# A row copy, two stack remainders and an exponential moved behind what TensorE waits for in the second FFN1 stage

## The chip, the core and the metric

The kernel runs on one core of one Trainium2 chip. The metric is the device time of one execution in microseconds, 1107.72 as the median of three runs before the change. TensorE (PE) multiplies matrices into eight banks of PSUM, VectorE (DVE) and ScalarE (ACT) do the elementwise work, GpSimd (POOL) and SyncE (SP) here mostly issue DMAs. ACT issues some DMAs too, in its own instruction order.

## The reference

The block adds attention and a feed-forward network, both on the same normalized input. Attention has 32 heads of 18 columns; each token looks at 8 tokens, at distances 0, 2, ..., 14 behind it. S is 2048, D 576 and F 4608.

```python
xn = _layernorm(x)                                   # x: (1, 2048, 576)
q, k, v = split_heads(xn @ wqkv)                     # 32 heads of 18
idx = pos[:, None] - 2 * jnp.arange(8)[None, :]      # masked where negative
logits = jnp.einsum("bhsd,bhswd->bhsw", q, k[idx]) * 18 ** -0.5
attn = softmax(logits)
o = jnp.einsum("bhsw,bhswd->bhsd", attn, v[idx])
h = xn @ w1 + b1                                     # 576 -> 4608
ffn = (relu(h) ** 2) @ w2 + b2                       # 4608 -> 576
return x + merge_heads(o) @ wo + ffn
```

## The kernel before

**Number format and blocks.** Tokens come in four blocks of 512 (0 to 3). Every fp32 operand of TensorE is split into a float32r high part, written by ScalarE (names ending in `_hi`), and the remainder, which VectorE forms by subtracting the high part (`_lo`). A product is then the sum of three matmuls: high times high and the two cross terms. FFN1 and QKV also use a Strassen-like scheme: two token blocks and two feature tiles are combined into seven products, by the names T1, T2, T3, T4, B11, B22 and B21, and rest columns go through a `left` product. Sums of weights and of inputs for it are formed beforehand.

**Order of the program.** All engines run in an order written out by hand: an engine executes its instructions in the order in which the Python code issues them, and waits at semaphores for other engines and DMAs. The order is: QKV of blocks 0 and 1; the first FFN1 stage (`phase_a(0)`: 18 pairs of feature tiles for blocks 0 and 1, with the FFN2 products of block 0 between); `phase_b0` (FFN2 of block 1, and then QKV of blocks 2 and 3, by `quads`, in four halves of 14 steps, here named (0,0), (0,1), (1,0) and (1,1)); the second FFN1 stage (`phase_a(1)`, blocks 2 and 3, with the FFN2 products of block 2), and `phase_b1` with the FFN2 products of block 3 and the end.

**One pair, `ffn_pair(s, p, work)`.** `s` is the stage and `p` the pair. It has three banks, ba, bb and bc. TensorE computes B11 into ba, ScalarE copies it into bb (L663); T1 goes into bc; T2 is added into bb, and ScalarE copies bb into `u[:, 0]` (L691). T3 is added into the same bb, so TensorE waits there for L691. ScalarE copies bb again (L723), and VectorE adds it to bc into `r1[:, 1]` (L725). VectorE's two-operand instructions are issued by a helper, so the profile puts them all on L108; this add reads `r<-p,r` there. B22 starts bc anew, so TensorE waits there for that add. B21, with its relu, stands between. `work(0)` to `work(3)` put FFN2 products (L536) of the pair before in between. In the first pair of stage 1, `work` is the function `filler`: `work(0)` issues the last quad step but one, (7,1), `work(1)` the last, (6,1), and later calls attention's output product. `splits()` issues the `_hi` and `_lo` parts of weights that the next pair needs. In pairs p > 1 of stage 1 the rest columns of several products are stacked in one tile of 32-row groups; pair p=1 prepares these stacks with `stack_hi` and `stack_lo`.

**A quad step's row.** Steps 4 to 7 each finish a row of q, k, v. `row` (L1047) lets ScalarE copy the bank into a slot of the tile `st` (L1050), of which there are four in turn, and for half of the rows VectorE adds another bank to it. A DMA then writes the slot to DRAM (L1054, `kvq<-st`), issued by ScalarE or, for rows with an add, by SyncE. The copy of a row waits until the DMA of the row four earlier has read its slot.

**Attention.** It is a generator for each pair of a block and a group of eight heads, (b, g), 17 pieces long: four times a multiply of q and k and a reduction (L387), one with the maximum and its subtraction, one with the exponential (ScalarE, L396), the sum, the reciprocal and the division, and four times a multiply with v and three adds, the last into `q`. `side(k, exp)` (L421) issues the next `k` pieces of the queue, and with `exp=False` stops ahead of an exponential. Pairs, quad steps and FFN2 loops call it at fixed places, so a piece more in one place moves every later piece of attention forward until the queue's next fixed point. Loads of k, v and q are issued by GpSimd (`fetch`, L347, at L358 and L360) as a buffer is released. When block 1's attention is done, GpSimd also loads its output in another grouping (`regroup`, L845).

Of the kernel before, what the change touches and what calls it, by code (L numbers as in the profile page):

```python
# [39 lines left out]
T1, T3, B11, T2, B22, B21, LEFT, T4 = range(8)  # L40
# [5 lines left out]
def block_kernel(ctx: ExitStack, tc: tile.TileContext, x, xt, wqkv, wo, w1, b1, w2, b2, w1l, out):  # L46
# [28 lines left out]
    half = const.tile([P, 1], F32, name="half")  # L75
# [31 lines left out]
    def tt(out, a, b, op):  # L107
        return nc.vector.tensor_tensor(out=out, in0=a, in1=b, op=op)  # L108
# [18 lines left out]
    def four(dt=F32):  # L127
        return sb.tile([P, 2, TB], dt, name="r4", bufs=4)
# [292 lines left out]
    def side(k, exp=True):  # L421

        while k > 0:
            if current[0] is None:
                if not queue or queue[0][0] not in landed:
                    return k
                name, make = queue.pop(0)
                current[:] = [make(), None, name]
            if current[1] == "exp" and not exp:
                return k  # L430
            try:
                current[1] = next(current[0])
                k -= 1
            except StopIteration:
                current[0] = None
        return 0
# [38 lines left out]
    def w1_hi(n, k):  # L475
        w1s[n, k] = mt.tile([P, 2, 4, 2 * P], F32R, name="w1s", bufs=3)
        nc.scalar.activation(w1s[n, k][:, 0], raw1[n][:, 4 * k:4 * k + 4], AF.Copy)  # L477
# [66 lines left out]
    ST, LW, LR = {}, {}, {}  # L544
# [16 lines left out]
    def stack_hi(to, v):  # L561
        nc.scalar.activation(to, v, AF.Copy)

    def stack_lo(to, v):
        rows = slice(L, 2 * L)
        tt(to[rows], v[rows], to[rows].bitcast(F32), ALU.subtract)
# [27 lines left out]
    def left_weight_hi(p):  # L594
        nc.scalar.activation(LW[p % 2], LR["w"], AF.Copy)

    def left_weight_lo(p):
        rows = slice(2 * L, P)
        tt(LW[p % 2][rows], LR["w"][rows], LW[p % 2][rows].bitcast(F32), ALU.subtract)
        load_left_weights(p + 1)  # L600
# [4 lines left out]
    def ffn_pair(s, p, work, first=False):  # L605
        b0, b1 = 2 * s, 2 * s + 1
        n = s * NP + p
# [23 lines left out]
        def left(to, f, v):  # L631
            if stacked:
                return
            for k in range(2):
                nc.tensor.matmul(to, weight(LEFT, k, f), v, start=False, stop=k == 1, skip_group_check=True)  # L635
# [45 lines left out]
            stack_hi(LR["st"][:, 0:2], LR["a"][:, 0:2])  # L681
            stack_hi(ST[T4], LR["a"][:, 3])
        if not first:
            side(1 if p == 1 else 3 if s else 2 + p % 2, s == 1)
        work(0)
        product(bb, T2, ss(2))
        own_w2 = first and s == 1
# [1 line left out]
            w2_hi()  # L689
        u = four()  # L690
        nc.scalar.activation(u[:, 0], bb, AF.Copy)  # L691
        if not first:
            left(bc, 1, x4[b1])
        work(1)
# [3 lines left out]
        def splits():  # L698
            if not own_w2:
                w2_lo()  # L700
            if not last and not s:
                w1_hi(n + 1, 0)
            if ready:
                left_weight_hi(p + 1)
            if s and p == 1:
                stack_lo(LR["st"][:, 0:2], LR["a"][:, 0:2])
                stack_lo(ST[T4], LR["a"][:, 3])
                stack_hi(ST[T1], LR["s"][:, 0])
            if not own_w2:
                w2_hi()  # L710
            if not last and not s:
                w1_lo(n + 1, 0)
            if ready:
                left_weight_lo(p + 1)
            if not own_w2:
                w2_lo()
# [6 lines left out]
        nc.scalar.activation(u[:, 1], bb, AF.Copy)  # L723
        r0, r1 = four(), four()
        tt(r1[:, 1], bc, u[:, 1], ALU.add)  # L725
        if first:
            splits()
        if not last and s:
# [297 lines left out]
    QKV_BANKS = [(2, 3, 4), (5, 6, 7)]  # L1026
    rows_out = [0]

    def quad_step(k, s, j, i):
        b0, b1, gs = 2, 3, (2 * k, 2 * k + 1)  # L1030
        a, b, c, u = [bank(n)[:, :QW] if opened is None else opened for n, opened in
                      zip((*QKV_BANKS[i], i), quad_banks[i])]
        quad_banks[i] = [a, b, c, u]
        js = slice(j * P, (j + 1) * P)

        def product(to, name, v, start=False):
            mm = [(v(0, n), ws[name][0][:, n]) for n in range(2)]
            for n in range(2):
                mm += [(v(0, n), ws[name][1][:, n]), (v(1, n), ws[name][0][:, n])]
            for n, (l, r) in enumerate(mm):  # L1040
                nc.tensor.matmul(to, l[:, js], r, start=start and n == 0, stop=n == len(mm) - 1, skip_group_check=True)  # L1041

        def left(to, f, v):
            for n in range(2):
                nc.tensor.matmul(to, v[:, js], ws[LEFT, f][:, n], start=False, stop=n == 1, skip_group_check=True)  # L1045

        def row(n, f, x, y=None):  # L1047
            st = stage[0][:, rows_out[0] % NJ]
            rows_out[0] += 1
            nc.scalar.activation(st, x, AF.Copy)  # L1050
            if y is not None:
                tt(st, y, st, ALU.add)
            to = kvq[gs[f]][:, PAD + n * TB:PAD + (n + 1) * TB].rearrange("i (p j) c -> p j i c", j=NJ)[:, j]
            (nc.sync if y is not None else nc.scalar).dma_start(to, st.rearrange("p (i c) -> p i c", c=CG))  # L1054

        ss = lambda n: lambda h, q: SS[n][:, h, q]
        if s == 1:
            product(a, B11, lambda h, q: X[b0][:, h, q], start=True)
            nc.scalar.activation(b, a, AF.Copy)
        if s == 2:  # L1060
            product(c, T1, ss(1), start=True)
        if s == 3:
            product(b, T2, ss(2))
            nc.scalar.activation(u, b, AF.Copy)
        if s == 4:
            left(c, 1, x4[b1])
            product(b, T3, ss(3))
            row(b1, 1, b, c)
        if s == 5:
            product(a, B21, lambda h, q: X[b0][:, h, 2 + q])  # L1070
            left(a, 0, x4[b0])
            row(b0, 0, a)
        if s == 6:
            product(c, B22, lambda h, q: X[b1][:, h, q])
            left(c, 1, x4["d"])
            row(b0, 1, c, u)
        if s == 7:
            product(b, T4, lambda h, q: X[b1][:, h, 2 + q])
            left(b, 0, x4[b1])
            row(b1, 0, b)  # L1080
# [3 lines left out]
    def phase_b0():  # L1084
# [99 lines left out]
                fetch()  # L1184

        steps = [(1, 0), (1, 1), (2, 0), (2, 1), (3, 0), (3, 1), (5, 0), (4, 0), (5, 1), (4, 1), (7, 0), (6, 0), (7, 1), (6, 1)]
        def quads(k, half, some):
            for n in some:
                s, i = steps[n]
                quad_step(k, s, 2 * half + i, i)  # L1190
                if n in ((2, 3, 4, 8, 10, 12), (3, 6, 10, 12), range(1, 13), (3, 6, 8, 10))[2 * k + half]:
                    side(1)
                hook(k, half, s, i)
# [5 lines left out]
        def chunks(*cs):  # L1199
            for c in cs:  # L1200
                w2_hi()
                add(b, o_ops(b, c))
                w2_lo()

        def filler(i):
            if i < 2:
                quads(1, 1, [len(steps) - 2 + i])
            if i == 1:
                load_left_rows()
                LR["w"] = sb.tile([P, 7, P], F32, name="mb")  # L1210
                load_left_weights(2)
                for g in (2, 3):
                    offer(2, g)
                for g in range(G):
                    offer(3, g)
            if i == 2:
                xr[b] = [mt.tile([P, NC - 1, TB], F32, name="h", bufs=3)]
                nc.sync.dma_start(xr[b][0], yscr)
                open_y(b)
                o_hi(b, 0), o_hi(b, 1)  # L1220
                o_lo(b, 0), o_lo(b, 1)
            if i == 2.5:
                o_hi(b, 2), o_hi(b, 3)
                chunks(0)
                o_lo(b, 2), o_lo(b, 3)
                chunks(1)
            if i == 3:
                open_left(b)
                nc.sync.dma_start(kept(b, NC - 1), yleft)
# [391 lines left out]
```

## Time and profile before

| what | value |
|---|---|
| median of three runs | 1107.72 us (1107.59 to 1108.0) |
| the profiled execution's own time | 1107.93 us |
| its span | 1106.2 us |
| granted TensorE clock in it | 1.00 |
| TensorE busy | 1096.8 us, 99% |
| VectorE busy | 912.0 us, 82% |
| ScalarE busy | 575.0 us, 52% |
| GpSimd busy | 115.4 us, 10% |
| DMA | 287.83 MB, 259 GB/s over the span |

A row of the timeline has the start in us from the beginning of the span, the length, the engine with its line (ACTq, SPq and POOLq are DMAs that this engine issues), the operation with output and input tiles, and how many instructions of one kind are put together. Brackets show how long the engine stood idle ahead of it and what released it. Lengths of matmuls overlap, so the time between two starts is what counts. In the trace, stage 0's second pair lies at about 111 to 129, the fourth half of the quads ends at 621.76, the first pair of the second stage begins there, its second pair has its add at 665.27, and the third its T3 at 680.16.

### The profile page before, as it was taken

The page shows a single profiled execution, that of the slowest core. Times are in us where ns is not written, and L with a number is a line of the kernel's source. Part 1 is how long each engine was busy: PE and PEld are TensorE (multiplying, and loading weights), DVE is VectorE, ACT ScalarE, POOL GpSimd, SP SyncE. Part 2 cuts the span into 40 slices and gives each one's busy share as a digit, 9 for nine tenths or more (in the row PEclk, how much of TensorE's full clock was granted, in tenths as well). Part 3 has the DMA queues.
Part 4 walks back from the last instruction along what each step waited for, and adds up shares of the span by engine and source line. Part 5 has one row for each costly group of instructions (what it writes and reads, how often), then busy time and mean ns, then how long its engine had stood idle before and what let it go on. Part 6 is the DMA issues. An engine that isn't in the chain of part 4 may idle for free.

```text
span 1106.2 us, 13892 instructions
## 1 busy us (share of the span) xinstructions
PE 1096.8 (99%) x4950; PEld 925.2 (84%) x4950; DVE 912.0 (82%) x1223; ACT 575.0 (52%) x809; POOL 115.4 (10%) x219
## 2 busy tenths in 40 slices
PE   9999999999999999999999999999999999999998
PEld 7998888888888888888899887888888888888887
DVE  7696979897996979999979488978988789899654
ACT  5435666556566654455344355555555555533342
POOL 4000101020020100100010200202102021000100
PEclk9999999999999999999999999999999999999999
DMA  8956987889699686866755887768686785866752
GB/s 297 329 177 234 333 309 255 296 214 372 229 244 392 220 357 214 311 247 226 259 164 169 309 263 300 259 260 308 238 315 240 267 314 205 316 208 205 280 193 81
DMA packets 100279, 287.83 MB, mean 260 GB/s; under 512 B 13288, under 2 KB 41712, under 8 KB 85488
## 3 DMA queue, kind: packets, MB, share of 16 engines
q1 hardware_dynamic: 65280, 188.15, 49.1%
q0 software_dynamic: 10544, 52.14, 12.9%
q10 hardware_dynamic: 24384, 46.64, 12.6%
q8 instruction: 39, 0.64, 0.2%
q14 instruction: 32, 0.26, 0.1%
HBM read 205.14 MB, written 81.74 MB: 259 GB/s over the span
## 4 chain that ended last, share of the span: by engine, by line
PE 89%; DVE 5%; DMA 3%; ACT 1%; issue 1%; ACTq 0%; POOL 0%; DVEq 0%; POOLq 0%; SPq 0%
PE p L536 46%; PE p L629 31%; PE p L1041 5%; PE p L635 3%; DMA kvq<-st 2%; PE p L338 1%; PE p L1401 1%; PE p L1045 1%; DVE pr L108 1%; DMA kv<-kvq 1%; DVE lg L387 1%; DVE w1r L108 1%; DVE r L108 0%; PE p L1318 0%; DVE h L108 0%
## 5 line engine op out<-in xcount | busy, mean ns | idle before, releaser
L536 PE MATMUL p<-h,w2s 128*128 128x512 f32 x2066 | 491.4, 389 | 0.1
L536 PEld LDWEIGHTS p<-h,w2s 128*128 128x128 f32 x2066 | 387.5, 188 | 81.5 <-ACT h L642 0.6
L629 PE MATMUL p<-X,w1s 128*128 128x512 f32 x864 | 219.7, 389 | 1.2 <-DVE r L108 0.9
L629 PEld LDWEIGHTS p<-X,w1s 128*128 128x128 f32 x864 | 162.0, 188 | 35.6 <-DVE r L108 1.3
L509 ACT ACTIVATE w2s<-w2r 128x640 fp32r<-128x640 f32 x164 | 120.2, 735 | 116.1 <-PE p L536 87.6
L629 PE MATMUL p<-S,w1s 128*128 128x512 f32 x648 | 164.8, 390 | 1.5 <-ACT r L691 1.5
L108 DVE TENSOR_TENSOR w2s<-w2r,w2s 128x576 fp32r<-128x576 f32 x164 | 123.4, 753 | 40.6 <-ACT w2s L509 39.8
L629 PEld LDWEIGHTS p<-S,w1s 128*128 128x128 f32 x648 | 121.4, 188 | 27.4 <-ACT r L691 2.3
L415 POOL DMA_DIRECT2D o<-q x128 | 69.2, 605 | 584.8 <-DVE q L108 582.8
L638 ACT ACTIVATE r<-r,b1t 128x512 f32<-128x512 f32 x72 | 52.0, 723 | 126.9 <-DVE r L108 125.2
L387 DVE TENSOR_REDUCE lg<-pr 128x64 f32<-128x1152 f32 x64 | 86.5, 1352 | 1.5
L108 DVE TENSOR_TENSOR pr<-lg,kv 128x1152 f32<-128x1152 f32 x64 | 86.7, 1354 | 1.3
L108 DVE TENSOR_TENSOR pr<-q,kv 128x1152 f32<-128x1152 f32 x64 | 86.6, 1353 | 0.8
L108 DVE TENSOR_TENSOR pr<-pr 128x576 f32<-128x576 f32 (+1 forms) x128 | 77.5, 605 | 3.2
L646 ACT ACTIVATE r<-r 128x1024 f32<-128x1024 f32 x72 | 76.1, 1057 | 1.2
L108 DVE TENSOR_TENSOR h<-r,h 128x1024 fp32r<-128x1024 f32 (+3 forms) x46 | 51.8, 1136 | 27.0 <-ACT r L646 18.8
L108 DVE TENSOR_TENSOR r<-p,r 128x512 f32<-128x512 f32 (+1 forms) x77 | 52.9, 688 | 20.3 <-PE p L629 9.8
L108 DVE TENSOR_TENSOR w1s<-w1r,w1s 128x1024 fp32r<-128x1024 f32 (+1 forms) x42 | 50.3, 1198 | 16.5 <-ACT w1s L477 16.4
L691 ACT ACTIVATE r<-p 128x512 f32<-128x512 f32 x36 | 21.5, 597 | 70.9 <-PE p L629 70.5
L638 ACT ACTIVATE r<-p,b1t 128x512 f32<-128x512 f32 x72 | 48.3, 672 | 0.0
L108 DVE TENSOR_TENSOR h<-h 128x1024 fp32r<-128x1024 f32 x36 | 43.9, 1220 | 4.8 <-ACT h L938 4.6
L536 PE MATMUL p<-w1s,w2s 128*128 128x512 f32 x195 | 44.7, 389 | 0.0
(193 smaller groups left out, 1174.2 us busy)
## 6 DMA issues: line engine op xcount, KB each, us to landing
w2r<-in_w SPq DMA_DIRECT2D x144, 320.0 KB, 3.4
kv<-kvq POOLq DMA_DIRECT2D x29, 1296.0 KB, 9.4
w<-w1s SPq DMA_DIRECT2D x36, 1024.0 KB, 8.4
w1s<-w ACTq DMA_DIRECT2D x34, 1024.0 KB, 7.3
h<-r SPq DMA_DIRECT2D x36, 512.0 KB, 6.3
h<-h SPq DMA_DIRECT2D x36, 512.0 KB, 4.2
w1r<-in_w SPq DMA_DIRECT2D x18, 640.0 KB, 7.7
kvq<-st ACTq DMA_DIRECT2D x48, 216.0 KB, 3.2
```

What stands on the lines that cost most here:

```text
L108: return nc.vector.tensor_tensor(out=out, in0=a, in1=b, op=op)
L338: nc.tensor.matmul(p[:, :QW], l, r, start=k == 0, stop=k == len(mm) - 1)
L387: nc.vector.tensor_reduce(out=lg[:, j * HG:(j + 1) * HG].rearrange("p a w -> p w a"), in_=pr.rearrange("p w (a d) -> p w a d", d=DH), axis ...
L415: nc.gpsimd.dma_start(rows[:, i], q[i * L:(i + 1) * L, :, a:z])
L509: nc.scalar.activation(w2s[stream[i]][:, :DE], raw2[i], AF.Copy)
L536: nc.tensor.matmul(yp[b][c], v, a, start=c not in yb[b], stop=c in last and c not in [o[0] for o in ops[i + 1:]], skip_group_check=True)
L629: nc.tensor.matmul(to, l, r, start=start and i == 0, stop=i == len(mm) - 1, skip_group_check=True)
L635: nc.tensor.matmul(to, weight(LEFT, k, f), v, start=False, stop=k == 1, skip_group_check=True)
L638: nc.scalar.activation(to, a, AF.Relu, bias=b1t[:, f:f + 1])
L646: nc.scalar.activation(r, r, AF.Square)
L691: nc.scalar.activation(u[:, 0], bb, AF.Copy)
L1041: nc.tensor.matmul(to, l[:, js], r, start=start and n == 0, stop=n == len(mm) - 1, skip_group_check=True)
```

## The change

There are three edits and one consequence of how the first is written.

1. The call of `side` ahead of T2. In stage 1, pair p=2 now gets one piece, without an exponential; it had three, with one allowed. The expression for "one piece" was `p == 1` in both stages, and is now `s and p in (1, 2)`. In stage 0, pair p=1 therefore falls to `2 + p % 2`, three pieces where it had one.
2. The row of quad step (7,1), which `filler` runs inside stage 1's first pair, is held back: its matmuls stay in place, but its copy and its DMA are issued by a new call `work(0.5)`, behind L691.
3. In stage 1's pair p=1 the two `stack_lo` calls (three VectorE instructions on 32 rows, of 1024 and 512 columns, beside others) move out of `splits()` to behind the add of `r1[:, 1]`.

```diff
         if not first:
-            side(1 if p == 1 else 3 if s else 2 + p % 2, s == 1)
+            side(1 if s and p in (1, 2) else 3 if s else 2 + p % 2, s == 1 and p != 2)
         work(0)
         product(bb, T2, ss(2))
...
         u = four()
         nc.scalar.activation(u[:, 0], bb, AF.Copy)
+        if s and first:
+            work(0.5)
...
             if s and p == 1:
-                stack_lo(LR["st"][:, 0:2], LR["a"][:, 0:2])
-                stack_lo(ST[T4], LR["a"][:, 3])
                 stack_hi(ST[T1], LR["s"][:, 0])
...
         tt(r1[:, 1], bc, u[:, 1], ALU.add)
+        if s and p == 1:
+            stack_lo(LR["st"][:, 0:2], LR["a"][:, 0:2])
+            stack_lo(ST[T4], LR["a"][:, 3])
...
         def row(n, f, x, y=None):
+            put = lambda: row_out(n, f, x, y)
+            held.append(put) if held is not None else put()
+
+        def row_out(n, f, x, y):
             st = stage[0][:, rows_out[0] % NJ]
...
         def filler(i):
-            if i < 2:
-                quads(1, 1, [len(steps) - 2 + i])
+            if i in (0, 1):
+                quads(1, 1, [len(steps) - 2 + i], None if i else held)
+            if i == 0.5:
+                held.pop()()
```

TensorE's and GpSimd's instructions keep their order. Three places show how the others move.

VectorE in stage 0's second pair, before: the end of an attention piece (`pr`, `q`), then remainders of weights, then the add into `r` that frees bc (`p` is a bank).

```order
L108 TENSOR_TENSOR pr<-pr 128x576
L108 TENSOR_TENSOR pr<-pr 128x288
L108 TENSOR_TENSOR q<-pr 128x144
L108 TENSOR_TENSOR w2s<-w2r,w2s 128x576
L108 TENSOR_TENSOR w1s<-w1r,w1s 128x1024
L108 TENSOR_TENSOR w2s<-w2r,w2s 128x576
L108 TENSOR_TENSOR r_1274<-p_1193,r_1242 128x512
```

The same place on VectorE in the changed kernel:

```order
L108 TENSOR_TENSOR pr<-pr 128x576
L108 TENSOR_TENSOR pr<-pr 128x288
L108 TENSOR_TENSOR q<-pr 128x144
L108 TENSOR_TENSOR pr<-q,kv 128x1152
L387 TENSOR_REDUCE lg<-pr 128x8x8
L108 TENSOR_TENSOR w2s<-w2r,w2s 128x576
L108 TENSOR_TENSOR w1s<-w1r,w1s 128x1024
L108 TENSOR_TENSOR w2s<-w2r,w2s 128x576
L108 TENSOR_TENSOR r_1280<-p_1193,r_1248 128x512
```

A multiply and a reduction of the next attention group now stand ahead of the weights' remainders and of the add.

ScalarE in stage 1's first pair, before (`p_4700` is the bank of step (7,1), `p_5310` is bb; the row of `w_113` is a DMA of weights):

```order
L663 ACTIVATE p_5310<-p_5309 128x512
L487 DMA w1s<-w_113 128x2048
L1050 ACTIVATE st<-p_4700 128x432
L1054 DMA kvq_98<-st 128x3x144
L691 ACTIVATE r_5344<-p_5310 128x512
L1050 ACTIVATE st<-p_4701 128x432
L723 ACTIVATE r_5344<-p_5310 128x512
```

The same place on ScalarE in the changed kernel, whose line numbers are a little higher behind the added lines:

```order
L663 ACTIVATE p_5325<-p_5324 128x512
L487 DMA w1s<-w_113 128x2048
L691 ACTIVATE r_5357<-p_5325 128x512
L1057 ACTIVATE st<-p_4728 128x432
L1061 DMA kvq_98<-st 128x3x144
L1057 ACTIVATE st<-p_4729 128x432
L723 ACTIVATE r_5357<-p_5325 128x512
```

The copy and the DMA of the held row have changed places with L691.

VectorE around the end of block 1's attention, before, in the fourth half of the quads: each quad half has four `st` adds, of its steps (4,0), (4,1), (6,0) and (6,1). The first two rows of this piece are the third half's last `st` add and the last multiply with v; the rows behind `q` belong to the fourth half and to attention (2,0).

```order
L108 TENSOR_TENSOR st<-p_4702,st 128x432
L108 TENSOR_TENSOR pr<-lg,kv 128x1152
L108 TENSOR_TENSOR pr<-pr 128x576
L108 TENSOR_TENSOR pr<-pr 128x288
L108 TENSOR_TENSOR q<-pr 128x144
L108 TENSOR_TENSOR st<-p_4690,st 128x432
L108 TENSOR_TENSOR pr<-q,kv 128x1152
L108 TENSOR_TENSOR st<-p_4701,st 128x432
L387 TENSOR_REDUCE lg<-pr 128x8x8
```

The end of block 1's attention on VectorE in the changed kernel; p_4718 takes the place of p_4690, and the first `st` add here is that of the third half's step (4,0):

```order
L108 TENSOR_TENSOR pr<-lg,kv 128x1152
L108 TENSOR_TENSOR st<-p_4718,st 128x432
L108 TENSOR_TENSOR pr<-pr 128x576
L108 TENSOR_TENSOR pr<-pr 128x288
L108 TENSOR_TENSOR q<-pr 128x144
L108 TENSOR_TENSOR pr<-q,kv 128x1152
L108 TENSOR_TENSOR st<-p_4729,st 128x432
```

And the last logit multiply of (2,0) there, between the third half's last `st` add and the fourth half's first:

```order
L108 TENSOR_TENSOR st<-p_4730,st 128x432
L387 TENSOR_REDUCE lg<-pr 128x8x8
L108 TENSOR_TENSOR pr<-q,kv 128x1152
L108 TENSOR_TENSOR st<-p_4718,st 128x432
L387 TENSOR_REDUCE lg<-pr 128x8x8
```

Block 1's last `q` add has moved ahead by three `st` adds, and the logits of (2,0), of which the first multiply stood in the fourth half, are done ahead of that half's end.

More of the change, by code (lines that the diff above doesn't have):

```diff
@@ L1027, in block_kernel, with quad_step @@
     rows_out = [0]
-    def quad_step(k, s, j, i):
+    def quad_step(k, s, j, i, held=None):
         b0, b1, gs = 2, 3, (2 * k, 2 * k + 1)
@@ L1186, in phase_b0, with quads @@
         steps = [(1, 0), (1, 1), (2, 0), (2, 1), (3, 0), (3, 1), (5, 0), (4, 0), (5, 1), (4, 1), (7, 0), (6, 0), (7, 1), (6, 1)]
-        def quads(k, half, some):
+        def quads(k, half, some, held=None):
             for n in some:
                 s, i = steps[n]
-                quad_step(k, s, 2 * half + i, i)
+                quad_step(k, s, 2 * half + i, i, held)
                 if n in ((2, 3, 4, 8, 10, 12), (3, 6, 10, 12), range(1, 13), (3, 6, 8, 10))[2 * k + half]:
@@ L1203, in chunks @@
                 w2_lo()
+        held = []
         def filler(i):
-            if i < 2:
-                quads(1, 1, [len(steps) - 2 + i])
+            if i in (0, 1):
+                quads(1, 1, [len(steps) - 2 + i], None if i else held)
+            if i == 0.5:
+                held.pop()()
             if i == 1:
```

## The prediction

> **What bounds the kernel now.** I began with the page's busy times and then asked for the waits of TensorE, since an engine that is busy 99% of the span can gain only where it stands still.
>
> ```profile
> PE 1096.8 (99%) x4950; PEld 925.2 (84%) x4950; DVE 912.0 (82%) x1223; ACT 575.0 (52%) x809; POOL 115.4 (10%) x219
> ```
>
> Of the four rows in the list of what TensorE waited for, these two are the change's stake (us in total, times, longest): two waits for L691, the copy of bb, which T3 then overwrites, and one for the add into `r`, which frees bc for B22.
>
> ```profile
> PE p L629 <- ACT r L691: 1.5, 2, 0.8
> PE p L629 <- DVE r L108: 0.9, 1, 0.9
> ```
>
> The timeline of TensorE shows where they lie (start, length, line, count, idle before), behind a piece of stage 0 that has no wait:
>
> ```profile
> 121.38 1.75 PE L536 MATMUL p<-h,w2s 128*128 128x512 f32 x7
> 122.96 1.52 PE L629 MATMUL p<-X,w1s 128*128 128x512 f32 x6
> 124.32 0.61 PE L635 MATMUL p<-x4d,w1s 128*128 128x512 f32 x2
> ...
> 628.82 0.55 PE L1045 MATMUL p<-r,x4d 128*128 128x432 f32 x2
> 630.21 1.65 PE L629 MATMUL p<-S,w1s 128*128 128x512 f32 x6 [0.85 <-ACT r L691]
> 631.70 0.70 PE L635 MATMUL p<-x,w1s 128*128 128x512 f32 x2
> ...
> 663.34 1.75 PE L536 MATMUL p<-h,w2s 128*128 128x512 f32 x7
> 666.02 1.65 PE L629 MATMUL p<-X,w1s 128*128 128x512 f32 x6 [0.93 <-DVE r L108]
> 667.51 0.62 PE L635 MATMUL p<-x4d,w1s 128*128 128x512 f32 x2
> ...
> 677.71 1.75 PE L536 MATMUL p<-h,w2s 128*128 128x512 f32 x7
> 680.16 1.66 PE L629 MATMUL p<-S,w1s 128*128 128x512 f32 x6 [0.70 <-ACT r L691]
> ```
>
> The lengths overlap, so I go by starts. Without a wait, seven matmuls of L536 take 1.58 (121.38 to 122.96) and six of L629 take 1.36 (122.96 to 124.32). The two of L1045, of 432 columns in place of 512, I put at 0.39. After a wait the six take 1.49 (630.21 to 631.70, 666.02 to 667.51), so a restart costs another 0.13.
>
> **The three gains.** First wait: T3 was due at 628.82 + 0.39 = 629.21 and came at 630.21, so 1.00, with the restart 1.13. Second: B22 was due at 663.34 + 1.58 = 664.92 and came at 666.02, so 1.10, with the restart 1.23. Third: due at 677.71 + 1.58 = 679.29, came at 680.16, so 0.87, with the restart 1.00. Sum: **3.36 us**.
>
> Does each go whole? ScalarE ahead of the two copies, from its timeline:
>
> ```profile
> 617.82 0.37 ACTq L1054 DMA_DIRECT2D kvq<-st  x1
> ...
> 628.59 0.53 ACT L1050 ACTIVATE st<-p 128x432 f32<-128x432 f32 x1 [4.46 <-DMA kvq<-st]
> ...
> 629.56 0.60 ACT L691 ACTIVATE r<-p 128x512 f32<-128x512 f32 x1 [0.44 <-PE p L1045]
> ...
> 678.58 0.42 ACT L396 ACTIVATE lg<-lg 128x256 f32<-128x256 f32 x1 [1.74 <-DVE lg L108]
> ...
> 679.53 0.58 ACT L691 ACTIVATE r<-p 128x512 f32<-128x512 f32 x1
> ```
>
> The row copy at 628.59 waited 4.46 us for its slot of `st`, whose DMA went out at 617.82, and L691 stood behind it. Put ahead of it, L691 runs as soon as T2 is done. Between T2 and T3 stand the eight matmuls of step (6,1), about 1.6 us, so T2 ends near 627.6 and L691 near 628.3, 0.9 us ahead of 629.21. The held copy then delays only its own bank, whose next use is an FFN2 product some microseconds on: cost 0, or at most its own 0.5 if that cover were gone.
>
> In the third wait the exponential at 678.58 waited 1.74 us for VectorE ahead of L691. With one piece and no exponential in p=2, L691 follows T2's last matmul, just ahead of the L536 group at 677.71, and ends near 678.3, 0.9 us ahead of its due time. Later exponentials fall in other pairs, since attention is some pieces ahead. In the list of waits, L691 appears twice, and only this once behind an exponential, so I price the others at nothing and bound each at this one's 1.0 us.
>
> VectorE before the second wait:
>
> ```profile
> 660.59 1.35 DVE L387 TENSOR_REDUCE lg<-pr 128x64 f32<-128x1152 f32 x1
> ...
> 662.64 1.82 DVE L108 TENSOR_TENSOR w1r<-w1r 32x1024 fp32r<-32x1024 f32 x2
> ...
> 665.27 0.69 DVE L108 TENSOR_TENSOR r<-p,r 128x512 f32<-128x512 f32 x1
> ```
>
> The two stack remainders are the 1.82. With these behind the add, it runs from 663.45 to 664.14, and B22 is due at 664.92: 0.8 of slack. The stacks are first multiplied in p=2, some ten microseconds on, which hides the remainders' own delay. The piece ahead of them becomes a multiply in place of L387, 1.35 like it (122.49 below).
>
> **The loss in stage 0.** The new condition asks for s=1, so stage 0's second pair falls through to three pieces where it had one. The two pieces, a multiply and a reduction, come ahead of four VectorE instructions, the last of which is the add that B22 needs:
>
> ```profile
> 115.27 1.60 DVE L108 TENSOR_TENSOR w1r<-w1r 128x512 f32<-128x512 f32 x3
> ...
> 120.76 0.68 DVE L108 TENSOR_TENSOR r<-p,r 128x512 f32<-128x512 f32 x1
> ...
> 122.49 1.35 DVE L108 TENSOR_TENSOR pr<-q,kv 128x1152 f32<-128x1152 f32 x1
> 123.88 1.35 DVE L387 TENSOR_REDUCE lg<-pr 128x64 f32<-128x1152 f32 x1
> 125.15 0.68 DVE L108 TENSOR_TENSOR r<-p,r 128x512 f32<-128x512 f32 x1
> ```
>
> VectorE is packed from 115.27 to 125, so they add 1.39 + 1.27 = 2.66 (122.49 to 125.15). The add then ends at 120.76 + 0.68 + 2.66 = 124.10. B22 started at 122.96 and now starts at 124.16 (at 666.02 it followed the add's end, 665.96, by 0.06): 1.20, with the restart **1.33 us**. The bounds are 0 and, if the add r0 behind is late as well, 2.66; I take the row's own sum.
>
> **What being ahead does to the DMAs.** By the order rows, block 1's last `q` add moves from the fourth QKV half to behind the p_4718 `st` add of the third. That row, the old place, and POOL's requests that follow:
>
> ```profile
> 598.80 0.60 DVE L108 TENSOR_TENSOR st<-p,st 128x432 f32<-128x432 f32 x1
> ...
> 612.21 0.31 DVE L108 TENSOR_TENSOR q<-pr 128x144 f32<-128x144 f32 x1
> ```
> ```profile
> 616.93 0.77 POOL L360 DMA_DIRECT2D kv<-kvq  x1
> ...
> 620.14 0.54 POOL L358 DMA_DIRECT2D q<-kvq  x1
> ...
> 672.26 0.53 POOL L360 DMA_DIRECT2D kv<-kvq  x1 [51.57 <-DVE pr L108]
> ```
>
> My estimate puts that add at 601.7 (598.80, and a multiply's lag and two adds), 10.5 sooner, so the burst of requests that began at 616.93 (v, the regrouping, q) begins at about 606.4. The load at 672.26 waited for the last logit multiply of (2,0), which the order puts ahead of the fourth half's first `st` add; it follows at about 613. What a burst does to a row's DMA, by issues (KB, us to landing: the rows issued at 616.89 and 617.82, POOL's q of 620.14, and a load of k at 583.04):
>
> ```profile
> kvq<-st SPq DMA_DIRECT2D x1, 216.0 KB, 2.4
> ...
> kvq<-st ACTq DMA_DIRECT2D x1, 216.0 KB, 10.7
> ...
> q<-kvq POOLq DMA_DIRECT2D x1, 288.0 KB, 8.6
> ...
> kv<-kvq POOLq DMA_DIRECT2D x1, 1296.0 KB, 8.0
> ```
>
> The row of 617.82 landed at 628.5, the burst's last request at 628.7: I take it that a row issued inside a burst lands when the burst ends. The burst lasted 11.8 (616.93 to 628.7) and would end at 618.2. The added load, requested at 613, would land at 621.0 by the 8.0 of its like, and at 626.2 if it only began at 618.2. Requests overlapped before, so I take a point a third of the way up, 622.6.
>
> Two row copies of the fourth half need slots whose DMAs go out at 614.69 and 616.89, inside that. The T1 product overwrites the bank of the second:
>
> ```profile
> 623.35 1.52 PE L629 MATMUL p<-S,w1s 128*128 128x512 f32 x6
> ```
>
> From 622.6 the two copies (0.53 each) end near 623.7, so T1 is 0.4 late, with the restart **0.5 us**. Bounds: 0 (landing before 622.2), and 5.0 by the 10.7 of the row above (the slower rival).
>
> The Trainium skill's page "DMA: Bandwidth & Descriptors", section "Queues, rings and completion order", says that each DMA engine takes turns between its queue rows, packet by packet. By that rule alone a small row would be served beside the burst and land well before its end; this term would be 0 and the time 1105.7. The trace speaks against an equal turn here: 10.7 us inside the burst against 2.4 at its start.
>
> **Sum.** -3.36 + 1.33 + 0.5 = -1.53. The profiled execution took 1107.93 (span 1106.2) and becomes 1106.4. The median of the runs, 1107.72, is 0.21 lower, so I predict 1106.2. A measurement of this kernel can tell about 0.2%, or 2.2 us, from no change; -1.53 lies within.
>
> **The rivals.**
>
> *The stage-0 pieces are hidden.* For it: stage 0's sixth pair has three pieces at this place and no wait:
>
> ```profile
> 183.22 1.60 DVE L108 TENSOR_TENSOR w1r<-w1r 128x512 f32<-128x512 f32 x3
> ```
> ```profile
> 193.68 1.52 PE L629 MATMUL p<-X,w1s 128*128 128x512 f32 x6
> ```
>
> Against it: there VectorE began the pair's w1r sums 10.5 us ahead of B22, here 7.7 (115.27 to 122.96), so it is 2.8 behind already, about the two pieces. Without the loss: -3.36 + 0.5 = -2.86, 1104.9. Chance 0.12.
>
> *Weights take the first wait's place.* The L635 behind T3 needs the weights that SP requested at 620.49:
>
> ```profile
> w1s<-w SPq DMA_DIRECT2D x1, 1024.0 KB, 11.1
> ```
>
> They landed at 631.6, 0.1 ahead of L635 at 631.70. If they come no sooner, L635 gains 0.1 and not 1.1: 1.0 is lost, 1107.2. The same price stands for a second exponential ahead of an L691. Against it: POOL's burst should by then be over, six us sooner than before. Chance 0.20.
>
> *The slower side: row copies hold T1.* Both copies also stand ahead of L663 and L691 in ScalarE's queue. If rows issued at 614.69 and 616.89 take the 10.7, the second lands at 627.6, its copy ends at 628.2, and T1 is 4.9 late, with the restart 5.0: -3.36 + 1.33 + 5.0 = +3.0, 1110.7. The change turns slower once the second row takes over about 7.2 us (624.1, T1 1.9 late). For it: the added load goes out just ahead of these rows. Against it: most of the burst is ten us older. Chance 0.16.
>
> That the change doesn't do what it says can't be: the order rows show L691 ahead of the copy.
>
> **How the numbers follow.** The forecast has 0.52, the rivals 0.12, 0.20 and 0.16. Faster by over 0.2%: the first rival's 0.12, and 0.15 of the forecast's, where rows land in time (-2.03) and another term is a little better: 0.27. Slower by over 0.2%: the last rival's 0.16. Within: 0.57. The range runs from 1104.7, just below the first rival, to 1108.6, the forecast with T1 2.4 us later, and leaves out most of the last rival.
>
> **What would show it.** In the profile after, TensorE's waits should hold no L691 and no `r` in stage 1, but one for `r` of some 1.2 near 123, and a short one for a row copy near 623 to 625. No wait near 123 makes the stage-0 term wrong. A wait for a weight DMA behind T3, or for L691 behind an exponential, is the second rival; one of 4 us or more ahead of T1 is the third. What would make all of it wrong is an attention schedule that, some pieces ahead, collides in a place that I haven't priced.

## The result, and the profile after

The changed kernel takes 1109.51 us (median of 18 runs, 1108.22 to 1113.55) against 1107.59 for the kernel before in the same rounds (18 runs, 1106.72 to 1108.55). The ratio is 1.0021, 95% interval 1.0014 to 1.0028: **slower by 1.5 to 3.1 us**, just at the bound of 0.2%. The prediction was 1106.2 with a range up to 1108.6, so the time lies above it, and the kernel became slower where a gain of 1.5 was forecast. The profiled execution took 1110.06, its span is 1108.4.

TensorE's waits in the changed kernel:

```profile
PE p L1329 <- DVE lg L1322: 2.1, 1, 2.1
PE p L629 <- DMA w1s<-w: 1.2, 1, 1.2
PE p L536 <- DVE w2s L108: 1.2, 1, 1.2
PE p L629 <- DVE r L108: 1.2, 1, 1.2
PE p L629 <- ACT st L1057: 0.6, 1, 0.6
PE p L662 <- ACT st L1057: 0.2, 1, 0.2
PE p L536 <- ACT h L941: 0.2, 1, 0.2
```

All three waits that the change aimed at are gone: no L691 is left, and the one `r` is another one. In their place stand six new ones (the first row is the opening's, and the kernel before has it too). The timeline of TensorE shows where, and also the three places that gained:

```profile
120.33 1.75 PE L536 MATMUL p<-h,w2s 128*128 128x512 f32 x7
123.23 1.66 PE L629 MATMUL p<-X,w1s 128*128 128x512 f32 x6 [1.16 <-DVE r L108]
...
477.33 23.04 PE L536 MATMUL p<-h,w2s 128*128 128x512 f32 x99 [0.17 <-ACT h L941]
...
546.90 2.56 PE L536 MATMUL p<-h,w2s 128*128 128x512 f32 x10 [1.22 <-DVE w2s L108]
...
625.90 1.66 PE L629 MATMUL p<-X,w1s 128*128 128x512 f32 x6 [1.24 <-DMA w1s<-w]
627.81 0.49 PE L662 MATMUL p<-X,w1s 128*128 128x512 f32 x1 [0.25 <-ACT st L1057]
628.86 1.65 PE L629 MATMUL p<-S,w1s 128*128 128x512 f32 x6 [0.56 <-ACT st L1057]
...
634.46 0.55 PE L1048 MATMUL p<-r,x4d 128*128 128x432 f32 x2
634.84 1.52 PE L629 MATMUL p<-S,w1s 128*128 128x512 f32 x6
...
667.71 1.75 PE L536 MATMUL p<-h,w2s 128*128 128x512 f32 x7
669.30 1.52 PE L629 MATMUL p<-X,w1s 128*128 128x512 f32 x6
...
680.86 1.75 PE L536 MATMUL p<-h,w2s 128*128 128x512 f32 x7
682.44 1.52 PE L629 MATMUL p<-S,w1s 128*128 128x512 f32 x6
```

T3 now follows L1048 by 0.38, and the L536 groups are followed after 1.59 and 1.58: no wait. The places where time was lost are stage 0's second pair (123), block 1's FFN2 loop (477 and 547), and the start of the second stage (624 to 629).

To add them up I compare the start of the same matmul in both traces. The table compares one execution of each kernel. Their openings differ (the first L1401 matmul at 7.66 before, its twin at 7.04 after), and just ahead of the first place the changed kernel is 1.04 ahead, so only changes of the difference count:

| place | before | after | difference | lost (+) or gained |
|---|---|---|---|---|
| B22, then x4d, stage 0 pair 1 | 122.96, 124.32 | 123.23, 124.73 | -1.04 ahead of it, +0.41 behind | +1.45 |
| first QKV step of blocks 2 and 3 | 546.56 | 549.30 | +2.74 (from +0.24 at 417.59) | +2.50 |
| first product of stage 1 | 621.76 | 625.90 | +4.14 | +1.40 |
| the step behind T1 | 624.71 | 630.35 | +5.64 | +1.50 |
| L635 behind T3 | 631.70 | 636.20 | +4.50 | -1.14 |
| x4d, stage 1 pair 1 | 667.51 | 670.66 | +3.15 | -1.35 |
| stack product behind T3, pair 2 | 681.66 | 683.80 | +2.14 | -1.01 |

Losses 6.85, gains 3.50; with the opening's -1.04 and a drift of -0.17 ahead of 417.59, the difference ends at +2.14, and the span grew by 2.2.

The sources lie in the other engines' timelines. In the FFN2 loop it is a load and the weights beside it: `w2r` is loaded, ScalarE forms its high part, and VectorE the remainder in `w2s`. Here are GpSimd's load, the high part, its remainder, and the last remainder of the loop, in the changed kernel and then in the kernel before:

```profile
458.44 0.54 POOL L360 DMA_DIRECT2D kv<-kvq  x1 [42.65 <-DVE w2s L108]
466.29 0.74 ACT L509 ACTIVATE w2s<-w2r 128x640 fp32r<-128x640 f32 x1 [6.45 <-DMA w2r<-in_w]
467.06 0.76 DVE L108 TENSOR_TENSOR w2s<-w2r,w2s 128x576 fp32r<-128x576 f32 x1 [3.73 <-ACT w2s L509]
546.10 1.42 DVE L108 TENSOR_TENSOR w2s<-w2r,w2s 128x576 fp32r<-128x576 f32 x2
```
```profile
534.65 0.54 POOL L360 DMA_DIRECT2D kv<-kvq  x1 [66.45 <-DVE pr L108]
463.78 0.74 ACT L509 ACTIVATE w2s<-w2r 128x640 fp32r<-128x640 f32 x1 [4.18 <-DMA w2r<-in_w]
464.55 0.76 DVE L108 TENSOR_TENSOR w2s<-w2r,w2s 128x576 fp32r<-128x576 f32 x1 [0.75 <-ACT w2s L509]
542.97 1.42 DVE L108 TENSOR_TENSOR w2s<-w2r,w2s 128x576 fp32r<-128x576 f32 x2
```

With attention ahead, a load of 1.3 MB that stood at 534.65 goes out at 458.44, while a w2r is under way. That w2r, requested at 455.17, took 11.0 us; its counterpart, requested at 454.93, took 8.7. From there on VectorE's remainders are 2.3 to 2.5 late, and in the loop's last rounds, where adds and multiplies of attention stand in place of the maximum, the exponential and the sum, the lag grows to 3.1 (546.10 against 542.97). TensorE stands until 546.90.

For the start of stage 1, here are GpSimd's requests, ScalarE, and the landings of the weights requested at 612.98, of the row issued at 617.43 and of the load of 615.38, all after:

```profile
608.60 0.76 POOL L360 DMA_DIRECT2D kv<-kvq  x1
...
613.63 0.54 POOL L358 DMA_DIRECT2D q<-kvq  x1
615.38 0.54 POOL L360 DMA_DIRECT2D kv<-kvq  x1 [1.20 <-DVE pr L108]
```
```profile
627.22 0.53 ACT L1057 ACTIVATE st<-p 128x432 f32<-128x432 f32 x1 [5.12 <-DMA kvq<-st]
627.78 0.37 ACTq L1061 DMA_DIRECT2D kvq<-st  x1
628.27 0.53 ACT L1057 ACTIVATE st<-p 128x432 f32<-128x432 f32 x1 [0.52 <-ACT st L1057]
```
```profile
w1s<-w SPq DMA_DIRECT2D x1, 1024.0 KB, 12.9
...
kvq<-st ACTq DMA_DIRECT2D x1, 216.0 KB, 9.7
...
kv<-kvq POOLq DMA_DIRECT2D x1, 1296.0 KB, 10.9
```

The weights landed at 612.98 + 12.9 = 625.9, where the first product starts. The row issued at 617.43 landed at 627.1, 0.9 behind the load that landed at 626.3, and the next one, issued at 619.64, at 627.4. The two copies at 627.22 and 628.27 let L662 and then T1 go, with a DMA that ScalarE issues between them. The copies don't wait for the weights, and the second ends at 628.80, so T1 would have come at 628.86 with weights in time too: the table's 1.40 and 1.50 are one loss of 2.9, and the rows set it.

### The profile page after: what moved, and what is told of

Same layout as the page of the kernel before. It is cut to its first block, busy times and chain, and to the rows that moved or that the text cites. A ratio compares the mean times of both kernels' runs of the same rounds, so it can differ in the third digit from the quotient of the medians.

```text
span 1108.4 us, 13891 instructions
## 1 busy us (share of the span) xinstructions
PE 1097.2 (99%) x4950; PEld 924.7 (83%) x4950; DVE 912.6 (82%) x1223; ACT 575.2 (52%) x809; POOL 115.9 (10%) x219
## 4 chain that ended last, share of the span: by engine, by line
PE 91%; DVE 4%; DMA 3%; issue 1%; ACT 1%; ACTq 0%; POOL 0%; DVEq 0%; POOLq 0%
PE p L536 42%; PE p L629 32%; PE p L338 7%; PE p L1044 5%; PE p L635 3%; DMA w2r<-in_w 1%; PE p L1048 1%; DVE w2s L108 1%; DMA kvq<-st 1%; PE p L1412 1%; DMA h<-r 0%; DVE pr L108 0%; DVE h L108 0%; DVE w1s L108 0%; DVE r L108 0%
## 5 line engine op out<-in xcount | busy, mean ns | idle before, releaser
L536 PE MATMUL p<-h,w2s 128*128 128x512 f32 x2066 | 492.3, 389 | 1.5 <-DVE w2s L108 1.2
L536 PEld LDWEIGHTS p<-h,w2s 128*128 128x128 f32 x2066 | 387.2, 188 | 84.1 <-DVE w2s L108 2.0
L629 PE MATMUL p<-X,w1s 128*128 128x512 f32 x864 | 219.5, 389 | 2.4 <-DMA w1s<-w 1.2
L629 PEld LDWEIGHTS p<-X,w1s 128*128 128x128 f32 x864 | 162.0, 188 | 36.7 <-DMA w1s<-w 1.6
L629 PE MATMUL p<-S,w1s 128*128 128x512 f32 x648 | 164.6, 389 | 0.6 <-ACT st L1057 0.6
L629 PEld LDWEIGHTS p<-S,w1s 128*128 128x128 f32 x648 | 121.5, 188 | 25.9 <-ACT st L1057 0.9
L691 ACT ACTIVATE r<-p 128x512 f32<-128x512 f32 x36 | 21.5, 598 | 73.1 <-PE p L629 73.1
L536 PE MATMUL p<-w1s,w2s 128*128 128x512 f32 x195 | 44.7, 389 | 0.0
```

Of the source, the lines that this page charges most:

```text
L536: nc.tensor.matmul(yp[b][c], v, a, start=c not in yb[b], stop=c in last and c not in [o[0] for o in ops[i + 1:]], skip_group_check=True)
L629: nc.tensor.matmul(to, l, r, start=start and i == 0, stop=i == len(mm) - 1, skip_group_check=True)
```

## The experiments

My theory after this result: the three edits do what they were meant to, and all that is lost comes from stage 0's second pair having three pieces instead of one, a little directly and most through attention being ahead. The rivals, for the experiments as a whole, were that one of the edits loses something itself, and that the pieces only cost where they stand. Each kernel was run against the kernel before in the same rounds; ratios with 95% intervals.

**e1_one_piece**, the changed kernel with stage 0 as it was:

```diff
-            side(1 if s and p in (1, 2) else 3 if s else 2 + p % 2, s == 1 and p != 2)
+            side(1 if p == 1 or s and p == 2 else 3 if s else 2 + p % 2, s == 1 and p != 2)
```

> The changed kernel with one piece of attention again in stage 0's second pair, all three edits kept. Theory (the two extra pieces cause every loss: directly at 123, by a DVE lag near 547, and by GpSimd's earlier loads near 626): the list of TensorE's waits holds none of the six new ones, and only the gains stay, about 3.4 us under the kernel before, 1104.2, ratio 0.997. Rival (the weights that SP requests at 620.49 take the first wait's place): a DMA wait of some 1 us behind T3, 1105.2. Rival (one of the three edits itself loses): above 1107.

Measured: 1105.46 against 1107.9, ratio 0.9977 (0.9968 to 0.9986). Behind the opening's wait, and beside one of 0.2 for `h` near 112, its list holds:

```profile
PE p L635 <- DMA w1s<-w: 0.9, 1, 0.9
```

None of the six is left, so the one expression makes the difference between +0.21% and -0.23%. But the first rival of its expectation holds too: the wait for the weights behind T3 takes the first wait's place. They were requested at 619.68 and took 11.1 us, as in the kernel before.

**e3_given_back** and **e4_ahead_in_pair2** part the direct loss from being ahead:

```diff
 e3
+            side(1 if s and p in (1, 2) else 3 if s else 0 if p == 2 else 2 + p % 2, s == 1 and p != 2)
 e4
+            side(1 if p == 1 or s and p == 2 else 3 if s else 4 if p == 2 else 2 + p % 2, s == 1 and p != 2)
```

> The changed kernel with three pieces in stage 0's second pair and none ahead of T2 in its third, so that attention is level with the kernel before from the third pair on. Theory (being ahead, not the two pieces themselves, costs most): only the wait of 1.2 near 123 is left, gains 3.4 less 1.4, about 1105.6. Rival (the lag of VectorE from the second pair goes on by itself): waits in the following pairs and near 547 stay, 1108 or more.

> The changed kernel with one piece in stage 0's second pair and four ahead of T2 in its third, so that attention is as far ahead from there on as in the changed kernel, but not by pieces at 118 to 121. Theory: no wait of 1.2 near 123 (at most 0.8 one pair later), and the losses near 477, 547 and 626 stay, about 1.4 under the changed kernel, 1108.1 to 1108.9. Rival (the pieces in the second pair cause all by themselves): 1104.2.

Measured: e3 1107.39, ratio 0.9994 (0.9986 to 1.0003); e4 1110.21, ratio 1.0018 (1.0009 to 1.0027). TensorE's timeline in e3, the rows with a wait at the two places, and e4's waits:

```profile
124.34 0.97 PE L629 MATMUL p<-X,w1s 128*128 128x512 f32 x3 [1.13 <-DVE r L108]
...
633.53 0.74 PE L635 MATMUL p<-x,w1s 128*128 128x512 f32 x2 [1.06 <-DMA w1s<-w]
```
```profile
PE p L629 <- DMA w1s<-w: 1.4, 1, 1.4
PE p L536 <- DVE w2s L108: 1.2, 1, 1.2
PE p L629 <- ACT st L1057: 0.6, 1, 0.6
PE p L536 <- ACT h L941: 0.4, 1, 0.4
```

With attention level again, only the direct wait is left, and e1's wait for weights, which explains most of what e3 lies above the expected time. With attention ahead by the same two pieces, but put into the next pair, the direct wait is gone and the others are there but for the short one of L662. So being ahead makes these waits, and by the table it is the larger part: 5.4 of 6.85. The time of e4 was not as expected: it should have been some 1.4 under the changed kernel, and by its ratio it can't be told from it. Its runs spread from 1108.25 to 1111.93, and the profiled one, 1108.98, is among the shorter ones.

**e2_three_only**, the kernel before with the three pieces alone:

```diff
-            side(1 if p == 1 else 3 if s else 2 + p % 2, s == 1)
+            side(1 if s and p == 1 else 3 if s else 2 + p % 2, s == 1)
```

> The kernel before with three pieces in stage 0's second pair and none of the three edits. Theory (the pieces alone cost all): waits of 1.2 near 123, about 0.2 and 1.2 near 477 and 547, and 2 near 626 for weights and row copies, as in the changed kernel; the waits for r and for L691 behind the exponential stay in stage 1, perhaps moved, and the one for L691 near 630 goes, since T1 comes late. 4 to 6 above the kernel before, 1111.8 to 1114. Rival (part of the loss comes from the edits): 1109.5 or less.

Measured: 1112.75, ratio 1.0048 (1.0036 to 1.006), 4.0 to 6.6 slower. Its waits of the same kinds:

```profile
PE p L629 <- DVE r L108: 2.4, 2, 1.3
...
PE p L536 <- DVE w2s L108: 1.2, 1, 1.2
PE p L629 <- DMA w1s<-w: 1.0, 1, 1.0
```

With two more for the row copies, of 0.5 and 0.4, the pieces alone make every loss. One of the two waits for `r` is the new one near 123; the other stands one pair later than before, at 689. The waits for L691 are gone as well, though no edit is in. For the one behind the exponential this was not expected: with attention ahead the exponential runs at 652.89, long before the third pair's L691 at 681.52. In the changed kernel it runs at 652.86, so there, too, being ahead would have removed that wait; whether the third edit does more there, at 689, was not tested.

**e7_held_only, e8_stack_only, e9_exp_only**, each of the three edits alone on the kernel before (e9's line is e1's):

```diff
 e7
+        if s and first:
+            work(0.5)
 e8
+        if s and p == 1:
+            stack_lo(LR["st"][:, 0:2], LR["a"][:, 0:2])
+            stack_lo(ST[T4], LR["a"][:, 3])
 e9
+            side(1 if p == 1 or s and p == 2 else 3 if s else 2 + p % 2, s == 1 and p != 2)
```

> The kernel before with the held row copy alone. Theory: the wait for L691 near 630 goes, and a wait of about 0.9 for the weights of L635 takes its place, so 0.1 to 0.3 is gained, 1107.6. Rival (my sum): 1.1 is gained, 1106.8.

> The kernel before with the two stack remainders moved alone. Theory: the wait for r near 666 goes and nothing comes for it, 1.2 gained, 1106.7. Rival (the remainders delay what stands behind them): a new wait in that pair or the next, 1107.4 or more.

> The kernel before with one piece and no exponential in pair 2 of stage 1 alone, stage 0 as before. Theory: the wait for L691 near 680 goes and no other exponential costs, 1.0 gained, 1106.9. Rival (the exponential only costs elsewhere, in a later pair): a wait for L691 in a later pair, 1107.9.

Measured: e7 1108.06, ratio 1.0 (0.9991 to 1.0008); e8 1106.3, ratio 0.9986 (0.9977 to 0.9995); e9 1107.43, ratio 0.9995 (0.9987 to 1.0004). In e9's list of waits the L691 of 680 is gone and none is new in stage 1; in e7's the L691 of 630 is gone, and a wait of 0.8 for the weights of L635 has come. The remainders' move gives its 1.2 (measured 0.6 to 2.5). The held copy alone gives nothing that can be told. For the exponential the trace shows the wait gone, but the interval of the time includes no change.

**e10_late_k**, the changed kernel with the loads of k (1296 KB) and q (288 KB) of (2,1) issued by SyncE behind its last row, so not within the burst:

```diff
 def regroup(b, k):
-            kept_back[0] = 0
+            kept_back[0] = 1
...
-            if kept_back[0] and not due(1):
+            if kept_back[0] and not due(1) and (1, 0) not in ob:
...
             if i == 1:
+                kept_back[0], lane[0] = 0, nc.sync
+                fetch()
+                lane[0] = nc.gpsimd
```

> The changed kernel with the load of k and q of attention (2,1) issued by SyncE behind its last row, near 636, not by GpSimd near 614. Theory (this load lengthens GpSimd's burst, and with it the landing of the first weights and of the two rows): the waits at 625.9, 627.8 and 628.9 go or shrink below 0.5 us, 2.4 to 2.9 under the changed kernel, about 1106.8. Rival (the burst's older part is enough, or the weights were late by their own request): at least 1.2 of these waits stay, 1108.4 or more.

Measured: 1108.14 (1106.67 to 1109.93), ratio 1.0004 (0.9995 to 1.0013). The start of the second stage in its trace:

```profile
625.03 0.55 PE L1048 MATMUL p<-r,x4d 128*128 128x432 f32 x2
625.41 1.52 PE L629 MATMUL p<-X,w1s 128*128 128x512 f32 x6
626.77 0.39 PE L662 MATMUL p<-X,w1s 128*128 128x512 f32 x1
627.00 1.52 PE L629 MATMUL p<-S,w1s 128*128 128x512 f32 x6
```

All three waits are gone, while those of 123 and 547 stay. So the load that the change pulls from 672 to 615, with the q that goes with it, is what made the weights and the rows late; the rest of the burst alone does not. The q was in the burst before the change too, so the load is the new part, but e10 doesn't part the two. The ratio fell by 0.0017, 1.9 us, less than the 2.4 to 2.9 that were expected, but within the intervals.

**e12_less_at_end**, the changed kernel with one piece fewer in the loop's last round:

```diff
-                    run(pieces, 2 if n > 21 else 1 + n % 2)
+                    run(pieces, 1 if n == 32 else 2 if n > 21 else 1 + n % 2)
```

> The changed kernel with one piece in place of two in the last FFN2 iteration of block 1 that calls for pieces. Theory (the wait for w2s near 547 is VectorE's own load: a multiply of 1.35 stands just ahead of that remainder): the wait of 1.2 for w2s goes, the others stay, about 1.2 under the changed kernel, 1108.5. Rival (the remainder was late by a DMA of w2r, as the one near 477): the wait stays, 1109.7.

Measured: 1113.25, ratio 1.0048 (1.0036 to 1.006). The wait for w2s is gone as expected, so VectorE's work ahead of that remainder is part of it. This doesn't rule out the late w2r, since VectorE had been late since 467, and a piece less makes up for part of that lag. The time was not as expected: by the ratios some 3 longer than the changed kernel instead of 1.2 shorter. TensorE's timeline:

```profile
626.40 0.49 PE L662 MATMUL p<-X,w1s 128*128 128x512 f32 x1
629.95 2.51 PE L629 MATMUL p<-S,w1s 128*128 128x512 f32 x6 [3.05 <-ACT st L1057]
632.25 2.09 PE L1044 MATMUL p<-h,X 128*128 128x432 f32 x6
```

One piece less put v 1.9 later, at 610.45, and the load of k 5.7 later, at 621.07, and the second row, issued at 619.54, then took 9.7 us: T1 was due at 626.63 and came at 629.95, 3.3 late. With a further 1.7, which the last section explains, this is 5.0, the price of the prediction's slower rival. The row that holds T1 is the rival's, but that the number agrees is chance: the rival had T1 4.9 late and no slower clock.

**e11_late_v, e13_weights_sooner, e14_both** start from e1_one_piece and go for its wait for weights: e11 lets SyncE load v of (2,0) behind its last row, e13 requests the weights three quad steps sooner (612.83 in place of 619.68), and e14 does both.

```diff
 e11: fetch() and filler(1)
+            if (kind, b, g) == ("k", 2, 0):
+                kept_back[0] = 2
...
-            kept_back[0] = 0
...
-            if kept_back[0] and not due(1):
+            if kept_back[0] and not due(1) and (1, 0) not in ob:
...
+                kept_back[0], lane[0] = 0, nc.sync
+                fetch()
+                lane[0] = nc.gpsimd
 e13: the hook of the fourth half
+                if (s, i) == (5, 0):
+                    w1_again(NP, 1, nc.sync)
...
-                if (s, i) == (4, 1):
-                    w1_again(NP, 1, nc.sync)
```

> e1_one_piece with the load of v of (2,0), 1296 KB, issued by SyncE behind its last row near 630 in place of GpSimd near 616. Theory (GpSimd's burst makes the weights requested at 619.7 late, which cost 0.9 behind T3): the DMA wait on L635 goes, and some 0.9 to 1.0 is gained on e1_one_piece, 1104.4, about 3.4 under the kernel before. Rival (the weights are late by the row DMAs and ScalarE's own 1 MB request): the wait stays, 1105.4.

> e1_one_piece with the second weight request of the second stage issued by SyncE two steps sooner, near 613, ahead of GpSimd's burst. Theory (the request of 619.7 was late by that burst): the DMA wait of 0.9 on L635 goes, 1.0 under e1_one_piece, 1104.5, ratio to the kernel before 0.9967. Rival (the megabyte then makes the rows late, and T1 with them): a wait for row copies near 623 in its place, 1105.5 or more.

> e1_one_piece with both remedies: the load of v of (2,0) by SyncE near 630, and the second weight request near 613. Theory (the request of 619.7 inside GpSimd's burst is all that is left of the first wait): no wait in the second stage, about 0.9 under e1_one_piece, 1104.5. Rival (TensorE's waits in the QKV and FFN2 loops vary from run to run by as much): the median is not to be told from e1_one_piece's, 1105.0 to 1105.9.

Measured: e11 1105.04, ratio 0.9975 (0.9966 to 0.9984); e13 1105.83, ratio 0.9985 (0.9977 to 0.9994); e14 1104.58, ratio 0.9972 (0.9962 to 0.9983). In all three the wait for the weights is gone from the profile. But other waits stand in the profiled executions, at places that none of these edits touches: one of 0.7 for w2s near 545 in e14, and this one in stage 0 of e11 (L631 and L693 are L629 and L691 there):

```profile
331.73 1.65 PE L631 MATMUL p<-S,w1s 128*128 128x512 f32 x6 [1.69 <-ACT r L693]
```

So both remedies take the wait away, but neither can be told from e1 by its time, for the intervals overlap. Through stage 0 and the FFN2 loop e1, e11, e13 and e14 are the same program, so the wait at 331.73 comes from the execution, or from the chip it ran on, and not from an edit. The time of e13 is the one of its rival, though no wait for row copies is in its profile. e14, 0.28% under the kernel before, has the lowest ratio of all, and beats both kernels.

## Why the prediction was wrong

**The gains** were right to about a tenth: I had 1.13, 1.23 and 1.00, and the traces differ by 1.14, 1.35 and 1.01. The first came whole in the changed kernel because attention is ahead there, as the prediction's reason against its second rival had it: GpSimd's burst is over at 626.3, and the weights requested at 623.23 took 7.8 us and landed at 631.0, 5.2 ahead of the L635 at 636.20. In e10, too, where T1 isn't late, the L635 behind T3 doesn't wait. With attention level (e1, e7) the burst is at its old place, the weights take L691's place, which is the second rival, and the first edit gives close to nothing.

**The loss in stage 0** was right: I had 1.33 near 123, and it measured 1.45, with a wait of 1.16 in the row.

**The step that failed is "What being ahead does to the DMAs"**, in two ways. First, its term was 0.5 and measured 2.9. It had the requests in the right place (my 606.4 and 613 are 608.60 and 615.38 in a trace that runs 2.5 to 2.7 later there) and the right mechanism, rows held up by the burst, but the wrong size. I put the landing a third of the way between the load alone and the load behind the whole burst, which gives that load 9.6 us. It took 10.9, and the rows landed 0.9 behind it and not with it, so they came 1.8 later than I had them (627.1 less 2.7, against 622.6). I also set the two copies behind the landing at 0.53 each and left out the DMA that ScalarE issues between them: 1.7 us in place of 1.1. So T1 came 2.8 late and not 0.4. The first product's own weights fell into the same burst and took 12.9 us where they had taken 5.0, and I had no term for them either; here their wait lies within that of the rows.

Second, the step stopped there. The same two pieces move GpSimd's load from 534.65 to 458.44, into block 1's FFN2 loop, and I had no term for that loop at all; it lost 2.5. My closing sentence had named that (a collision in a place that I hadn't priced), but neither the sum nor the chances held it. GpSimd's list of loads, followed through the whole program, could have shown it.

**The rivals.** The slower one was right in its mechanism. The second row, issued at 619.64, took 7.8 us, a little over the turning point of 7.2, but it was the first, with 9.7, and the copy and the DMA behind it that set T1. Hidden pieces in stage 0 did not occur. The rows came 0.9 behind the end of GpSimd's load, and in e10, without that load, there was no wait. The Trainium skill's rule of turns ("DMA: Bandwidth & Descriptors", "Queues, rings and completion order"), as the prediction read it, would have let the rows land well before the load's end, and they did not. That speaks against the reading more than against the rule: the trace records a row as 384 pieces of 576 bytes and the load as 128 of 10368, so equal turns need not be equal shares. No run tests that.

**What stays open.** That the load at 458.44 makes the w2r late is read from the order in time; no run moves that load alone. For it: counted from the start of the FFN2 loop (417.59 and its twins), the remainder of 464.55 comes 2.3 to 3.1 later in all five kernels with attention ahead, and in the eight others between 0.3 sooner and 0.9 later. The whole loop takes 130.9 to 132.2 us in those five kernels and 129.0 to 130.1 in the others and the kernel before. Four places make up nearly all of the 2.5: by the starts of successive matmuls, 0.227 apart without a wait, TensorE loses 0.45 near 477, 0.25 near 497, 0.17 near 542 and 1.49 near 547. A wait for `h` of 0.17 to 0.43 near 477 stands in the five kernels with attention ahead and in none of the others. The w2s waits near 545 in e11, e13 and e14 have the same form with a smaller lag: counted in the same way, their remainder of 542.97 comes 1.1 to 1.5 later than before, where it is 0.7 at most in the level kernels without this wait. What makes VectorE late in these three I don't know; e1 is the same program there and has no such wait.

## What to carry to other kernels

Where side work is dealt out in pieces, one piece more in one place moves all that follows, and with it loads that start when a buffer is released: follow the moved loads to the end of the program and price each place where they meet another transfer with a deadline. When an expression's condition is rewritten, write out its value for every case, for here a branch for one stage changed the other and cost twice what the edits gained. And when a wait is removed, look for the transfer that had landed just ahead of its end, since that is what ends the next wait.

## What the runs showed of the hardware

A stall of TensorE can cost more than its length. In e12 TensorE stood from 626.6 to 629.95, 3.3 us, and the next six matmuls took 2.30 in place of 1.36 and the eight behind them 2.32 in place of 1.57, 1.7 us more. The granted clock of these stretches (each row has the stretch, its length, the busy times of PE, PEld, DVE, ACT and POOL, then the clock, the DMA share and GB/s):

```profile
629.00:631.00 2.00, 1.05 (x4) 0.85 (x5) 0.61 (x1) 1.02 (x2) 0.00 (x0) 0.87 1.03 423
631.00:632.00 1.00, 1.00 (x4) 0.81 (x3) 0.00 (x0) 0.00 (x0) 0.00 (x0) 0.50 1.02 360
632.00:634.00 2.00, 2.00 (x8) 1.80 (x7) 0.00 (x0) 0.00 (x0) 0.00 (x0) 0.53 1.04 427
634.00:636.00 2.00, 2.00 (x11) 1.72 (x10) 0.00 (x0) 0.00 (x0) 0.00 (x0) 1.00 0.52 176
```

The clock fell to half and came back: a mean of 0.87 over the first 2 us is a fall near 630.5, and one of 0.53 from 632 to 634 a return near 633.9, so it stood at half for some 3.4 us. The shorter stalls of the other kernels cost only about 0.13 beyond the delay of their first matmul, and around the longest, the 1.69 of e11, the clock stayed at 1.00. The Trainium skill's page "TensorE: Matmul & The Clock Gate", in "What's actually happening", gives half rate after an idle window of about 3.4 us and full rate after about as long a busy one; this one case is close to both, with a stall of 3.3 and 3.4 at half rate.

Executions of one kernel also differ: the changed kernel's 18 runs span 5.3 us, those of e8 (11 runs) 1.1. That waits come and go where the program is the same is seen in e11: its wait of 1.69 at 331.73 isn't there in e1, e13 or e14, each of which ran on another chip.
